# The first batch's attention with transposed scores, and its state read-out moved from slot 0 to slot 1

## The chip, the cores and the metric

One core of a Trainium2 chip runs the kernel. The metric is device time in microseconds (us). A profiled execution gives the span (first to last instruction), some 1.8 us under the device time. Engines: PE (matmul; PEld is its weight load), DVE (VectorE), ACT (ScalarE), POOL (GpSimd), SP (SyncE). A name with q, such as SPq, is that engine's instruction queue.

## The reference

Attention between 512 tokens and 32 state rows for each of 8 batches and 8 heads, in both directions, then a two-layer network with exact GELU over all 4,352 rows. It is cut to what matters:

```python
scores = scale * x @ state.T            # (B, H, 512, 32)
xread = softmax(scores, -1) @ state     # tokens read the state
sread = softmax(scores.T, -1) @ x       # the state reads the tokens: "read-out"
attn = concat([xread, sread], axis=2)   # (B, H, 544, 64); subtraction of maxima and 1e-9 left out
h = attn.transpose(0, 2, 1, 3).reshape(B * 544, 512) @ w_in      # 512 -> 2048
out = gelu_exact(h) @ w_out                                      # 2048 -> 512
```

## The kernel before

The kernel does not form `xread` by itself: it forms P = state · w_in for each batch, and the hidden layer is (normalised scores) · P. Both kinds of read share one set of exponentials `e`, laid out with tokens on the partitions: the normalised `a` is transposed to `AT` for the hidden products, and `e` itself is the left operand of the read-out `sr`. All 8 batches' read-outs go through the network together at the end. P is made piece by piece, as the pieces of w_in land; the products of its third piece are called the third P stretch. A row block is 128 rows of w_out.

Batch b's work on PE is called slot b. Weights come in pieces over GpSimd's one queue while slot 0 runs. What the change and the argument touch:

```python
    load_w_in(0, 512)            # two transfers (partition halves) of 256 KB
    load_w_out(0)                # first quarter of w_out, 512 KB
    load_w_in(512, 1024)
    load_st(1, 2)
    ...
    def load_rest():             # called later in the start
        load_x(1)
        load_w_out(1)            # second quarter
        for f in range(2, FC):
            load_w_in(512 * f, 512 * f + 512)
            load_w_out(f)
    ...
    def scores0(q):              # batch 0, two heads of each half at a time: tokens on partitions
        pc = ps_o.tile([128, SJ, 2 * NS], FP32, name="pc", tag="op")
        for j in range(SJ):
            nc.tensor.matmul(pc[:, j, :], lhsT=xT0[:, q, j, :], rhs=sb0[...], ...)
        nc.scalar.activation(out=part0(A.e, q), in_=pc, func=AF.Exp, scale=scale)
    # sums0: reduce_sum on DVE; norm0: reciprocal, then a = e * (1/sum) on GpSimd (t=0) or DVE (t=1);
    # atr(0): eight PE transposes of a, two copies to AT
    ...
    pmat00(0)                    # P, first piece: 4 products, ACT copies them
    nc.scalar.activation(out=gate, in_=gate, func=AF.Gelu)   # loads the GELU table early
    ...
    pmat00(1)
    ...                          # eight hidden products, four GELUs, then products with w_out
    # slot 0, later:
    M(6); begin(1); xtr(1, (0, 1)); xtr(1, (2, 3))
    sread(0)                     # read-out: 32 products of 32 columns
    sread_out(0)                 # reciprocal and multiplication on DVE
    M(7); scores(1, 0); scores(1, 1)
    srt(0)                       # transpose of the read-out
    U(4, 5)                      # first products that need w_out's second quarter
    ...
    # M(m): two hidden products and their GELU; U(u): four products with w_out.
    # Tile pools in PSUM: ps_f and ps_o, four buffers each; hidden products, score tiles and sr turn through ps_f.
    ...
        if q == 3:               # a finished tile of 128 rows: copied and stored
            rows = out_rows(b, j)
            h = d_model // 2 if j == SJ - 1 else d_model      # the last tile of a batch in two stores
            evac(ps, [(rows[:, n:n + h], slice(0, 128), n, n + h) for n in range(0, d_model, h)])
```

The softmax here doesn't subtract the row's maximum and nothing guards it: scores larger than these inputs give would overflow.

## Time and profile before

| | before |
|---|---|
| time, median of 3 runs | 215.44 us (215.35 to 215.75) |
| span of the profiled execution | 213.6 us |
| first GELU of batch 0 starts | 12.67 us |
| first product with w_out's second quarter | 21.18 us |
| slot 0 ends (score products of the batch after next start) | 44.16 us |
| slot 1 ends (the same of the batch after) | 57.58 us |
| last output tile's products start | 206.99 us |

How to read it. The last rows are times at which PE passes the same piece of work in every version. Differences between two kernels in the distance from one such milestone to the next tell in which stretch time was gained or lost. The line behind 21.18 stands in the prediction, those behind the other milestones in the result. The chains shown there date a group of products some 0.17 us later than the timeline, from which the milestones are taken, because a chain's piece starts where the one before it ends.

### The profile page before, as it was taken

What the parts mean: (1) busy time and instruction counts of PE and PEld (TensorE: products, weight loads), DVE (VectorE), ACT (ScalarE), POOL (GpSimd) and SP (SyncE); (2) the same over time, 40 slices, a digit from 0 to 9 for tenths busy, and PEclk for the clock granted to TensorE, in tenths of its full rate; (3) what the DMA queues carried; (4) which work ended last, traced back from release to release, by engine and by line L of the source; (5) the groups of instructions that cost most, each with busy time, mean ns of one, the idle gap of its engine ahead of it and who ended that gap; (6) DMA issues with size and microseconds to landing.
All of it is one profiled execution on the core that took longest, in us unless ns stands there. A gap on an engine that the chain in (4) does not pass through costs nothing.

```text
span 213.6 us, 4028 instructions
## 1 busy us (share of the span) xinstructions
PE 209.2 (98%) x1674; PEld 103.7 (49%) x1674; DVE 81.3 (38%) x169; ACT 122.5 (57%) x218; POOL 43.5 (20%) x57
## 2 busy tenths in 40 slices
PE   8999999999999999999999999999999999999994
PEld 7735444444444445444444444444444444765443
DVE  3835675723059102940177006900393026000151
ACT  3765855797777448844974467645864444864000
POOL 7573304901213013302321230300000000000000
PEclk9999999999999999999999999999999999999999
DMA  7999999983722691439350963170222014000034
GB/s 182 172 200 205 206 193 161 220 178 51 96 98 101 122 123 50 150 60 144 47 196 4 155 90 139 60 146 5 98 100 54 0 40 158 3 0 0 10 105 183
DMA packets 39731, 22.98 MB, mean 108 GB/s; under 512 B 22048, under 2 KB 36384, under 8 KB 39712
## 3 DMA queue, kind: packets, MB, share of 16 engines
q0 software_dynamic: 13664, 8.23, 27.8%
q1 hardware_dynamic: 25360, 14.09, 24.6%
q10 hardware_dynamic: 688, 0.39, 0.6%
q8 instruction: 13, 0.21, 0.4%
q14 instruction: 6, 0.05, 0.1%
HBM read 17.30 MB, written 8.91 MB: 123 GB/s over the span
## 4 chain that ended last, share of the span: by engine, by line
PE 97%; POOL 0%; ACT 0%; issue 0%; DVE 0%
PE op L519 47%; PE hp L470 25%; PE p_ps L408 4%; PE op L564 3%; PE hps L534 3%; PE ops L546 3%; PE warm_ps L133 2%; PE opl L497 2%; PE pt L316 2%; PE sr L371 1%; PE hp L624 1%; PE aT_ps L353 1%; PE xT_ps L239 1%; POOL a L303 0%; PE xT_ps L258 0%; PE pc L279 0%
## 5 line engine op out<-in xcount | busy, mean ns | idle before, releaser
L519 PE MATMUL op<-w_out_bf,g 128*128 128x512 bf16 x464 | 110.1, 379 | 0.0
L477 ACT ACTIVATE g<-hp 128x512 bf16<-128x512 f32 x124 | 66.5, 600 | 52.8 <-PE hp L470 52.7
L519 PEld LDWEIGHTS <-g 128*128 128x128 bf16 x464 | 44.9, 98 | 54.3 <-issue 1.5
L470 PE MATMUL hp<-AT,P 128*128 128x512 bf16 x248 | 63.4, 379 | 0.0
L483 DVE COPY osb<-op 128x512 f32<-128x512 f32 x31 | 21.4, 691 | 85.0 <-PE op L519 85.0
L470 PEld LDWEIGHTS <-P 128*128 128x128 bf16 x248 | 22.8, 98 | 25.2 <-ACT P L419 0.5
L419 ACT CAST P<-p_ps 128x512 bf16<-128x512 f32 x31 | 16.3, 595 | 12.5 <-PE p_ps L408 12.5
L420 DVE CAST P<-p_ps 128x512 bf16<-128x512 f32 x31 | 19.9, 682 | 6.0 <-PE p_ps L408 5.9
L202 POOL COPY x<-xb 128x1024 bf16<-128x1024 bf16 x12 | 12.2, 1043 | 31.9 <-DMA xb<-in_x_dram 26.5
L212 POOL COPY xo<-xb 128x1024 bf16<-128x1024 bf16 x12 | 12.2, 1049 | 21.7 <-PE sr L371 21.7
L336 DVE TENSOR_REDUCE cs<-e 128x16 f32<-128x512 bf16 x14 | 9.5, 678 | 4.0 <-ACT e L323 4.0
L323 ACT ACT_TABLE_LOAD x7 | 9.0, 1283 | 1.8 <-issue 1.3
L408 PE MATMUL p_ps<-w_in_bf,sbd 64*32 64x512 bf16 x248 | 9.9, 381 | 0.0
L483 DVE COPY osb<-ops 128x512 f32<-128x512 f32 x2 | 1.4, 692 | 22.5 <-PE ops L546 22.5
L339 DVE TENSOR_TENSOR a<-e,ics 128x512 bf16<-128x512 bf16 x14 | 9.7, 692 | 0.5
L477 ACT ACT_TABLE_LOAD x7 | 9.0, 1283 | 0.1
L508 ACT COPY osb<-opl 128x128 f32<-128x128 f32 x1 | 0.3, 266 | 15.2 <-PE opl L497 15.2
L133 PE MATMUL warm_ps<-warm 128*128 128x128 bf16 x66 | 7.0, 275 | 1.0 <-DVE warm L80 1.0
L564 PE MATMUL op<-w_out_bf,g 128*128 128x512 bf16 x32 | 7.8, 380 | 0.0
L323 ACT ACTIVATE e<-pt 128x512 bf16<-128x512 f32 x14 | 7.6, 594 | 0.1
L534 PE MATMUL hps<-XSR,w_in_bf 128*128 128x256 bf16 x64 | 7.6, 273 | 0.0
L546 PE MATMUL ops<-w_out_bf,g_sr 128*128 128x512 bf16 x32 | 7.1, 379 | 0.0
(80 smaller groups left out, 118.9 us busy)
## 6 DMA issues: line engine op xcount, KB each, us to landing
out_dram<-osb SPq DMA_DIRECT2D x24, 256.0 KB, 2.3
xb<-in_x_dram POOLq DMA_DIRECT2D x7, 512.0 KB, 6.2
w_in_bf<-in_moe_w_in_dram POOLq DMA_DIRECT2D x8, 256.0 KB, 10.1
w_out_bf<-in_moe_w_out_dram POOLq DMA_DIRECT2D x4, 512.0 KB, 11.6
out_dram<-osb SPq DMA_DIRECT2D x14, 128.0 KB, 2.0
x0f<-in_x_dram SPq DMA_DIRECT2D x2, 256.0 KB, 3.5
out_dram<-osb SPq DMA_DIRECT2D x8, 64.0 KB, 1.7
x0f<-in_x_dram ACTq DMA_DIRECT2D x1, 256.0 KB, 4.2
```

The source lines that it names most:

```text
L202: nc.gpsimd.tensor_copy(out=A.x4[:, :, :, 64 * t:64 * t + 64].rearrange("p j c d -> p c j d"), in_=src[:, t],)
L323: nc.scalar.activation(out=A.e[:, :, 64 * half:64 * half + 64], in_=pt.rearrange("p j t c n -> p (j t) (c n)"), func=AF.Exp, scale=scale,)
L408: nc.tensor.matmul(ps[t][32 * c:32 * c + 32, :], lhsT=sbd[64 * t:64 * t + 64, b, c, 32 * t:32 * t + 32], rhs=w_in_bf[64 * t:64 * t + 64, c ...
L419: nc.scalar.copy(out=dst[:, 0, :], in_=ps[0])
L420: nc.vector.tensor_copy(out=dst[:, 1, :], in_=ps[1])
L470: nc.tensor.matmul(hp, lhsT=Ps[b][:, t, m * 128:(m + 1) * 128], rhs=atts[b].AT[:, :, t, :], start=(t == 0), stop=(t == 1),)
L477: nc.scalar.activation(out=gs[b][:, m, :], in_=hp, func=AF.Gelu)
L483: nc.vector.tensor_copy(out=osb, in_=ps)
L519: nc.tensor.matmul(ps, lhsT=gs[b][:, m, j * 128:(j + 1) * 128], rhs=w_out_bf[:, m, :], start=(m == 0), stop=(m == MC - 1),)
L534: nc.tensor.matmul(hp, lhsT=w_in_bf[:, c, m * 128:(m + 1) * 128], rhs=XSR[:, c, :], start=(c == 0), stop=(c == HC - 1),)
L546: nc.tensor.matmul(ps, lhsT=g_sr[:, m, s * 128:(s + 1) * 128], rhs=w_out_bf[:, m, :], start=(m == 0), stop=(m == MC - 1),)
L564: nc.tensor.matmul(ops[b, j], lhsT=gs[b][:, m, j * 128:(j + 1) * 128], rhs=w_out_bf[:, m, :], start=(m == 0), stop=(m == MC - 1),)
```

## The change

Its intent: shorten the way to the first hidden product. Batch 0's scores are computed with state rows on the partitions, which is the layout the hidden products want, so that the GpSimd normalisation, the eight transposes and two copies go. Sums come from products with a 0/1 matrix and are spread again by 32 broadcast products for each half of the heads. The read-out still wants tokens on partitions: its operand now comes from a DMA transpose of the exponentials, and the read-out moves to slot 1. The first piece of w_in comes in four transfers instead of two, and the casts and copies of x go to DVE.

```diff
-    load_w_in(0, 512)
+    load_w_in(0, 256, (0,))
+    load_w_in(256, 512, (0,))
+    load_w_in(0, 256, (1,))
+    load_w_in(256, 512, (1,))
     load_w_out(0)
@@ scores0: one product of 512 columns for each q, one exp for each pair
-        for j in range(SJ):
-            nc.tensor.matmul(pc[:, j, :], lhsT=xT0[:, q, j, :], rhs=sb0[...], ...)
-        nc.scalar.activation(out=part0(A.e, q), in_=pc, func=AF.Exp, scale=scale)
+        nc.tensor.matmul(pcs[t][h, :], lhsT=sb0[...], rhs=xT0[:, q, :, :]..., ...)
+        if q % 2 == 1:
+            nc.scalar.activation(out=eT0[:, t, :], in_=pcs[t], func=AF.Exp, scale=scale)
@@ sums0: four products with the 0/1 matrix, reciprocal, its low part
+            nc.tensor.matmul(ps[:, j, :], lhsT=eT0[:, t, 128 * j:128 * j + 128], rhs=bones, ...)
+        nc.vector.reciprocal(out=r0[:, t, :, :], in_=ps)
+        nc.vector.tensor_tensor(out=r0lo[...], in0=r0[...], in1=r0_hi(t), op=ALU.subtract)
@@ norm0: for each half 32 broadcast products, one multiplication from PSUM
+                    nc.tensor.matmul(ps[...], lhsT=r[:, j, c:c + 1].to_broadcast((128, NS)), rhs=ident, ...)
+        nc.vector.tensor_tensor(out=A.AT[:, :, t, :], in0=eT0[...], in1=ps..., op=ALU.mult)
+    def e0_dma():
+        nc.sync.dma_start_transpose(out=e0, in_=eT0.rearrange("p t s -> p (t s)"))
@@ start
+    load_rest()                  # now behind the scores, some 2 us sooner
     sums0(0)
+    pmat00(0)
+    nc.scalar.activation(out=gate, in_=gate, func=AF.Gelu)
     sums0(1)
     norm0(0)
     norm0(1)
     pmat00(1)
@@ slot 0
-    sread(0)
-    sread_out(0)
     M(7)
     scores(1, 0)
     scores(1, 1)
-    srt(0)
@@ behind batch 2's transpose, before slot 1
     xtr_dma(2)
+    e0_dma()
@@ slot 1, p == 4, behind the next batch's scores
+                    sread(0)
+                    sread_out(0)
@@ slot 1, p == 5
+                srt(0)
```

Left out: the removed lines of sums0, norm0, atr(0) and of the old start, the order of warm-up products, copies moved between ACT and DVE, new buffers, and the index of `e` in `sread`.

More of the change, by code (lines that the diff above doesn't have):

```diff
@@ L64 @@
     sb0 = persist.tile([128, 2, 2, 2, NS], BF16, name="sb0")
+    e0 = persist.tile([128, 2 * SJ, 128], BF16, name="e0")
+    eT0 = persist.tile([128, 2, S], BF16, name="eT0")
+    xo0 = persist.tile([128, SJ, HC, 132], BF16, name="xo0")
+    bones = persist.tile([128, HC], BF16, name="bones")
+    r0 = persist.tile([128, 2, SJ, HC], FP32, name="r0")
+    r0lo = persist.tile([128, 2, SJ, HC], BF16, name="r0lo")
     gate = persist.tile([128, HC], FP32, name="gate")
@@ L85, with load_w_in @@
     nc.vector.memset(sb0, 0.0)
-    for i in range(2):
-        nc.vector.memset(xos[i][:, :, :, 1:2], 1.0)
-        nc.vector.memset(xos[i][:, :, :, 130:131], 1.0)
-    def load_w_in(f0, f1):
-        for t in range(2):
+    nc.vector.memset(bones, 0.0)
+    for c in range(HC):
+        nc.vector.memset(bones[32 * c:32 * c + 32, c:c + 1], 1.0)
+    for xo in xos + [xo0]:
+        nc.vector.memset(xo[:, :, :, 1:2], 1.0)
+        nc.vector.memset(xo[:, :, :, 130:131], 1.0)
+    def load_w_in(f0, f1, ts=(0, 1)):
+        for t in ts:
             nc.gpsimd.dma_start(
@@ L127, in load_rest, with keep_warm @@
         load_x(3)
-    def keep_warm(n):
-        ps = ps_o.tile([128, 512], FP32, name="warm_ps", tag="op")
+    warm_ps = ps_o.tile([128, 512], FP32, name="warm_ps", tag="op")
+    def keep_warm(n, m=128):
         for _ in range(n):
-            nc.tensor.matmul(ps[:, 0:128], lhsT=warm, rhs=warm, start=True, stop=True)
+            nc.tensor.matmul(
+                warm_ps[0:m, 0:128], lhsT=warm[:, 0:m], rhs=warm, start=True, stop=True
+            )
     def state_prep(b0, b1):
@@ L171, in state0 @@
             h = slice(64 * u, 64 * u + 64)
-            nc.vector.tensor_copy(out=sb0[h, :, :, u, :], in_=ps[h, 0:2, u:HC:2, :])
+            nc.scalar.copy(out=sb0[h, :, :, u, :], in_=ps[h, 0:2, u:HC:2, :])
         return ps
@@ L189, in begin @@
         A.x4 = x4s[b % 2]
-        A.xo = xos[b % 2]
-        if b > 0:
-            A.xT = att.tile([128, SJ, HC, 128], BF16, name="xT", tag="xT")
+        A.xo = xos[b % 2] if b else xo0
+        if b == 0:
+            A.e = e0
+            A.AT = att.tile([128, SJ, 2, 128], BF16, name="AT", tag="AT")
+            return
+        A.xT = att.tile([128, SJ, HC, 128], BF16, name="xT", tag="xT")
         A.e = att.tile([128, SJ * 2, HC * NS], BF16, name="e", tag="e")
@@ L218, in cast0 @@
     def cast0(q):
-        copy = nc.scalar.copy if q == 1 else nc.vector.tensor_copy
-        copy(
+        nc.vector.tensor_copy(
             out=x0b[:, q, :, :, :].rearrange("p j u d -> p u j d"),
@@ L246, in xtr0 @@
                 )
-        copy = nc.scalar.copy if q == 2 else nc.vector.tensor_copy
-        copy(out=xT0[:, q, :, :], in_=ps)
+        nc.vector.tensor_copy(out=xT0[:, q, :, :], in_=ps)
     def xtr(b, cs):
@@ L268, in xtr_dma, with sums0 @@
         )
-    def part0(x, q):
-        v = x.rearrange("p (j t) f -> p j t f", t=2)[:, :, q // 2, :]
-        return v[:, :, 64 * (q % 2):64 * (q % 2) + 64]
+    pcs = {}
     def scores0(q):
-        A = atts[0]
-        pc = ps_o.tile([128, SJ, 2 * NS], FP32, name="pc", tag="op")
+        t = q // 2
+        if q % 2 == 0:
+            pcs[t] = ps_o.tile([128, S], FP32, name="pc", tag="op")
+        h = slice(64 * (q % 2), 64 * (q % 2) + 64)
+        nc.tensor.matmul(
+            pcs[t][h, :],
+            lhsT=sb0[:, t, q % 2, :, :].rearrange("p u n -> p (u n)"),
+            rhs=xT0[:, q, :, :].rearrange("p j n -> p (j n)"),
+            start=True,
+            stop=True,
+        )
+        if q % 2 == 1:
+            nc.scalar.activation(out=eT0[:, t, :], in_=pcs[t], func=AF.Exp, scale=scale)
+    def sums0(t):
+        ps = ps_f.tile([128, SJ, HC], FP32, name="cs0", tag="f")
         for j in range(SJ):
             nc.tensor.matmul(
-                pc[:, j, :],
-                lhsT=xT0[:, q, j, :],
-                rhs=sb0[:, q // 2, q % 2, :, :].rearrange("p u n -> p (u n)"),
+                ps[:, j, :],
+                lhsT=eT0[:, t, 128 * j:128 * j + 128],
+                rhs=bones,
                 start=True,
@@ L285, in scores0, with r0_hi @@
             )
-        nc.scalar.activation(out=part0(A.e, q), in_=pc, func=AF.Exp, scale=scale)
-    def sums0(q):
-        A = atts[0]
-        if q % 2 == 0:
-            A.sums = att.tile([128, SJ, HC], FP32, name="cs", tag="cs")
-        nc.vector.reduce_sum(
-            out=A.sums[:, :, q % 2 * 2:q % 2 * 2 + 2],
-            in_=part0(A.e, q).rearrange("p j (c n) -> p j c n", n=NS),
-            axis=AX.X,
-        )
+        nc.vector.reciprocal(out=r0[:, t, :, :], in_=ps)
+        nc.vector.tensor_tensor(
+            out=r0lo[:, t, :, :], in0=r0[:, t, :, :], in1=r0_hi(t), op=ALU.subtract
+        )
+    def r0_hi(t):
+        v = r0.rearrange("p t j c -> p (t j c)").bitcast(BF16)
+        return v.rearrange("p (t j c w) -> p t j c w", t=2, j=SJ, w=2)[:, t, :, :, 1]
     def norm0(t):
         A = atts[0]
-        ics = att.tile([128, SJ, HC], FP32, name="ics", tag="ics")
-        nc.vector.reciprocal(out=ics, in_=A.sums)
-        eng = nc.gpsimd if t == 0 else nc.vector
-        eng.tensor_tensor(
-            out=A.a.rearrange("p (j t) (c n) -> p j t c n", t=2, n=NS)[:, :, t, :, :],
-            in0=A.e.rearrange("p (j t) (c n) -> p j t c n", t=2, n=NS)[:, :, t, :, :],
-            in1=ics[:, :, :].to_broadcast((128, SJ, HC, NS)),
+        ps = ps_o.tile([128, S], FP32, name="rb", tag="op")
+        for j in range(SJ):
+            for i, r in enumerate((r0_hi(t), r0lo[:, t, :, :])):
+                for c in range(HC):
+                    nc.tensor.matmul(
+                        ps[32 * c:32 * c + 32, 128 * j:128 * j + 128],
+                        lhsT=r[:, j, c:c + 1].to_broadcast((128, NS)),
+                        rhs=ident,
+                        start=(i == 0),
+                        stop=(i == 1),
+                    )
+        nc.vector.tensor_tensor(
+            out=A.AT[:, :, t, :],
+            in0=eT0[:, t, :].rearrange("p (j n) -> p j n", j=SJ),
+            in1=ps.rearrange("p (j n) -> p j n", j=SJ),
             op=ALU.mult,
         )
+    def e0_dma():
+        nc.sync.dma_start_transpose(out=e0, in_=eT0.rearrange("p t s -> p (t s)"))
     def scores(b, half):
@@ L372, in sread @@
                         A.sr[32 * c:32 * c + 32, t, :],
-                        lhsT=A.e[:, 2 * j + t, 32 * c:32 * c + 32],
+                        lhsT=A.e[:, 2 * j + t if b else SJ * t + j, 32 * c:32 * c + 32],
                         rhs=A.xo[:, j, c, 1 + 65 * t:66 + 65 * t],
@@ L583 @@
     cast0(0)
+    xtr0(0)
     st0 = state0()
-    xtr0(0)
     cast0(1)
     state0_p(st0)
-    keep_warm(7)
+    keep_warm(9)
     cast0(2)
     xtr0(1)
+    keep_warm(2)
+    xtr0(2)
+    xtr0(3)
     scores0(0)
-    xtr0(2)
-    keep_warm(4)
     scores0(1)
+    keep_warm(1, 64)
+    scores0(2)
+    keep_warm(2, 64)
+    scores0(3)
+    load_rest()
     sums0(0)
-    xtr0(3)
-    keep_warm(2)
-    scores0(2)
-    keep_warm(4)
+    pmat00(0)
+    nc.scalar.activation(out=gate, in_=gate, func=AF.Gelu)
     sums0(1)
     norm0(0)
-    scores0(3)
-    sums0(2)
-    sums0(3)
     norm0(1)
-    load_rest()
-    keep_warm(8)
-    pmat00(0)
-    nc.scalar.activation(out=gate, in_=gate, func=AF.Gelu)
-    keep_warm(5)
-    atr(0, (0,))
-    keep_warm(4)
     pmat00(1)
-    atr(0, (1,))
     for q in range(4):
@@ L723 @@
                 srt(b)
+            if p == 5 and b == 1:
+                srt(0)
     while u < 16 * B - 4:
```

## The prediction

> **What bounds the kernel now.** I read the busy shares first, then the chain that ended last, then the order of time of the first 25 us, then the DMA issues in short windows. From the page:
>
> ```profile
> PE 209.2 (98%) x1674; PEld 103.7 (49%) x1674; DVE 81.3 (38%) x169; ACT 122.5 (57%) x218; POOL 43.5 (20%) x57
> ...
> PE 97%; POOL 0%; ACT 0%; issue 0%; DVE 0%
> ```
>
> PE is the bound from beginning to end: after the start every microsecond that PE neither loses nor gains elsewhere arrives at the end. So the change is worth (a) how much earlier the first batch's hidden products begin, (b) waits that it adds or removes on PE later. The chain of waits, from 8 us on:
>
> ```profile
> 8.77 0.39 ACT e L286
> 9.16 1.05 POOL a L303
> 10.21 0.05 issue
> 10.25 0.40 PE aT_ps L353 x4
> ...
> 11.53 1.75 PE hp L624 x8
> ...
> 18.75 1.01 PE xT_ps L258 x32
> 19.77 0.36 PE sr L371 x31
> 20.12 0.54 PE hp L470 x2
> 20.66 0.47 PE pt L316 x16
> 21.13 0.21 PE srT L395
> ```
>
> The only stretch not carried by PE is 8.77 to 10.25: the last exp, then GpSimd's normalisation (1.05). That is what the change attacks. But a second path runs beside it, on ACT, in the order of time:
>
> ```profile
> 9.55 0.59 ACT L460 CAST P<-p_ps 128x512 bf16<-128x512 f32 x1 [0.40 <-PE p_ps L453]
> ...
> 10.16 1.28 ACT L609 ACT_TABLE_LOAD   x1
> ...
> 11.45 0.20 ACT L609 ACTIVATE gate<-gate 128x4 f32<-128x4 f32 x1
> 11.56 0.57 ACT L460 CAST P<-p_ps 128x512 bf16<-128x512 f32 x1
> ```
>
> The second P copy ends at 12.13; the second half of the eight hidden products loads its weights at 12.18, released by that copy. So ACT (P copy, GELU table, P copy) is already as late as the attention path, and stays after it.
>
> The third thing to see is the load stream. Every weight comes over GpSimd's one queue, busy without a break to 37 us. The output projection's second quarter is issued at 11.10 and takes 10.0 us:
>
> ```profile
> w_out_bf<-in_moe_w_out_dram POOLq DMA_DIRECT2D x1, 512.0 KB, 10.0
> ...
> 21.18 1.02 PE L519 MATMUL op<-w_out_bf,g 128*128 128x512 bf16 x4
> 21.42 0.99 POOL L104 DMA_DIRECT2D xb<-in_x_dram  x1 [1.92 <-DMA w_out_bf<-in_moe_w_out_dram]
> ```
>
> It lands at 21.14; its first product starts at 21.18. PE was ready just then by itself, so it costs nothing today, but there is no slack: whatever PE gains before 21 us it will spend waiting here. By the same arithmetic other slacks are: first quarter of w_out 12.2 against 13.3, second piece of w_in 15.3 against 16.0, batch 1's x 18.2 against 18.7, third piece 23.3 against 23.9.
>
> **What the Trainium skill says.** "ScalarE: Activation LUTs", section "What ACT_TABLE_LOAD costs", gives about 1283 ns for a load, whatever the set, and 186 ns + 0.833 ns a column for an ACTIVATE. The trace agrees: 1283 ns a load, 597 ns for 512 columns (613 by that formula), 388 for 256. Two exps of 512 columns thus cost 1.2 us where four of 256 cost 1.6. "TensorE: Matmul & The Clock Gate", "Part 3: Packing small matmuls — row/col tiling", says that products of 32 columns in different column groups overlap; here 32 read-out products start within 0.24 us (19.70 to 19.93), so it agrees. The same page's "Part 1: The HAM clock gate" puts the warm clock after some 4 us of activity and its loss after an idle window of about 3.4 us; here products of 128 columns go from 107 to 56 ns apart near 6.6 us, and the new gaps are all well under a microsecond, so I expect no cold stretch. "DMA: Bandwidth & Descriptors", "Specifications", has 512 B as the least size for line rate. The trace shows a small loss even there, by stretch:
>
> ```profile
> 19.00:23.00 4.00, 4.00 (x88) 2.57 (x83) 2.92 (x7) 2.72 (x4) 2.08 (x3) 1.00 1.24 205
> 32.40:34.60 2.20, 2.20 (x11) 0.84 (x9) 0.00 (x0) 1.30 (x3) 0.00 (x0) 1.00 1.46 200
> 5.50:8.20 2.70, 2.70 (x45) 2.48 (x44) 2.00 (x6) 1.92 (x6) 1.10 (x2) 1.00 1.10 146
> ```
>
> The last number is GB/s. The first stretch moves 1024-byte packets at 205; the second 512-byte packets, at 191 when the 0.02 MB of instruction fetch is left out.
>
> **The change, part by part.** Times are the span's.
>
> *Scores transposed.* Sixteen products of 64 columns become four of 512 (216 ns each warm, from the hidden products' spacing). x's transposes come first on PE (4.38 instead of 4.9), all casts and transposed copies go to DVE at 0.42 each. DVE in order: cast 0 to 4.27, copy 0 5.05 to 5.48, cast 1 to 5.91, cast 2 to 6.35, copy 1 6.89 to 7.31 (after nine warm-up products at 107 ns), copy 2 to 7.75, copy 3 to 8.19. First exp from 7.87 to 8.45; the fourth score product needs copy 3, starts at 8.26 and ends at 8.64; second exp 8.67 to 9.25. Before, the last exp ended at 9.15: nothing gained yet.
>
> *Sums and normalisation.* Four products for the sums (0.3), reciprocal 0.25, subtraction about 0.1, 32 broadcast products (eight steps of 56 ns, 0.45, plus 0.17 until they have landed), one multiplication from PSUM 0.7. First half: sums done 8.95, reciprocal and low part 9.35, broadcast 9.6 to 10.25, multiplied 10.97. Second half: sums 9.3 to 9.6, low part 10.0, broadcast 10.1 to 10.7, multiplied 11.7. The GpSimd pass (1.05), eight transposes (0.8) and two copies (0.84) go.
>
> *ACT.* The first P copy can start at 9.28, when the second exp ends, instead of 9.55. Then 0.59, table 1.28, gate 0.11 before the copy may follow, copy 0.57: end at 11.86 instead of 12.13. The first four hidden products run 11.0 to 11.9, the second four from 11.95. **The start gains 0.27 us**, set by ACT; attention at 11.7 lies just under it.
>
> *Read-out moved.* Leaves slot 0 with 0.36 + 0.21 of the chain. There, though, the second score tile then waits for the second transposed copy of x (0.68 on DVE), so about 0.3 is freed.
>
> *The w_in split.* Four loads of 512-byte rows for two of 1024: 524 kB at 191 instead of 205 GB/s is 2.75 for 2.56 us, +0.2 on every later landing. GpSimd's issues rise by 2 x 0.63 us, and the rest is issued about 2 us sooner; both are hidden, as the queue is never empty.
>
> *Put together at w_out's second quarter.* PE would be ready 0.3 + 0.27 earlier, at about 20.6; the data lands at 21.14 + 0.2 = 21.34, products at 21.38. So slot 0 ends **+0.2 us**, its 0.57 gained turned into a wait.
>
> *Read-out in slot 1.* After 44 us PE is full, so it is paid: 0.36 for the 32 products and 0.06 for the transpose (0.06 is what that costs in later slots, where it waits for nothing). It also takes a PSUM buffer of the four that the hidden products turn through. Score tiles hold two until exp, which sits behind a table load:
>
> ```profile
> 44.64 1.28 ACT L323 ACT_TABLE_LOAD   x1 [0.37 <-PE pt L316]
> ...
> 45.93 1.08 ACT L323 ACTIVATE e<-pt 128x512 bf16<-128x512 f32 x2
> ```
>
> The second hidden product of that step therefore needs the read-out's own buffer or a score tile's. If it is the read-out's: products land about 45.13, reciprocal 0.16 and multiplication 0.29 with gaps to 45.66, PE ready at 45.4 and starting at 45.7: a wait of about 0.25. **Sum for slot 1: 0.36 + 0.06 + 0.25 = +0.65.** The DMA transpose of e is issued near 39 us and should take the 3.2 us of its like of the same eight blocks, so it lands near 42.5, before 44.7; stores behind it have time.
>
> *Total.* +0.2 + 0.65 = +0.85; on 215.44 that is 216.3. I take 216.2, as the kernel's author kept such a step presumably for a reason.
>
> **Rivals.**
> 1. *The gain stands.* If the first loads come faster split than whole, w_out lands sooner. For it: the stretch 5.5 to 8.2 moves only 146 GB/s, 0.16 MB or 0.8 us behind the later rate, and it is exactly the piece that is split. Against: nothing in the profile says that packet size is the reason. Then slot 0 ends up to 0.5 earlier, total about 215.5 to 215.7.
> 2. *The score tile's buffer is taken.* Then the hidden product waits for the first exp, 46.53 + 0.05, against 45.41: 1.15 instead of 0.25, total about 217.2. For it: the tiles turn over in order. Against: in the compiled kernel before, slot 0's transposed read-out gives its bank on before the older score tiles do, so banks follow the expected release.
> 3. *A slower load stream.* If small rows also lengthen that slow stretch, landings slip by 0.5 or more, and each of the near deadlines becomes a wait: about 216.7 to 217.
> 4. *Attention sets the start instead of ACT*, if the broadcast products or the multiplications from PSUM run longer: hidden up to 0.5 us by the same w_out wait.
>
> **Range and chances.** Rival 1 with a smaller slot 1 gives the low side, 215.2; rival 2 or 3 the high side, 217.2. Two per cent is 4.3 us, beyond any sum of these: faster 0.01, within 0.975, slower 0.015.
>
> **What would show it.** Second P copy ending near 11.9, first GELU near 12.4 instead of 12.67; the first L519-like products with g of batch 0 and the second quarter of w_out starting within 0.1 us of its landing, with PE idle before; read-out products near 45 followed by a wait of a quarter microsecond before the second hidden product; PE busy about 0.5 us lower in slot 0. It is wrong if w_out's landing moves by more than 0.4 us either way, if PE's wait in slot 1 ends with an exp, or if the clock falls in the start.

## More of the kernel before

Differences of a few tenths of a microsecond are near the spread of single runs (the kernel before, on one chip, lay between 214.95 and 216.69 in eleven runs), so the argument rests on intervals of repeated rounds for the times and on profiles for the places.

## The result

| | before | changed |
|---|---|---|
| time, median | 215.59 us (215.35 to 215.99, 4 runs) | 216.58 us (216.40 to 216.82, 4 runs) |
| span of the profiled execution | 213.6 us | 215.0 us |

The ratio is 1.0045, 95% interval 1.0025 to 1.0064. Ratios in this document are the mean time of one kernel's fast runs over that of the kernel before in the same rounds, so they are not quite the ratios of the medians. The changed kernel's profiled run was the slowest of its four; its milestones run some 0.4 us late against the repeat below, the first product with w_out's second quarter 0.85.

First the page of the changed kernel, the chain that ended last, by engine:

```profile
PE 88%; DMA 6%; POOL 3%; issue 1%; DVE 0%; ACT 0%; POOLq 0%
```

Before, this line began with 97% for PE. Now 6% of the span, some 12.5 us, is a DMA: the chain goes back from the first product with w_out's second quarter to that transfer, and from there to GpSimd's issues of the loads in front of it. By this chain no work of PE, ACT or DVE before 21 us is on the path any more. The timeline of the changed kernel shows both ends of that statement, first on ACT (start, length, line, operation; in brackets the idle time before it and what ended it), then on PE, with the issue-to-landing time of the transfer from the list of DMA issues in the third fence. The fourth is the kernel before's first GELU:

```profile
9.74 1.28 ACT L643 ACT_TABLE_LOAD   x1
...
11.14 0.57 ACT L500 CAST P<-p_ps 128x512 bf16<-128x512 f32 x1
...
12.19 2.06 ACT L665 ACTIVATE g<-hp 128x512 bf16<-128x512 f32 x4 [0.48 <-PE hp L657]
```

```profile
21.33 2.75 PE L559 MATMUL op<-w_out_bf,g 128*128 128x512 bf16 x11 [0.48 <-DMA w_out_bf<-in_moe_w_out_dram]
```

```profile
w_out_bf<-in_moe_w_out_dram POOLq DMA_DIRECT2D x1, 512.0 KB, 12.5
```

```profile
12.67 2.06 ACT L632 ACTIVATE g<-hp 128x512 bf16<-128x512 f32 x4 [0.54 <-PE hp L624]
```

The table load starts 0.42 earlier (9.74 for 10.16), the second P copy ends at 11.71 for 12.13, and the first GELU starts 0.48 earlier. Then PE waits 0.48 for w_out's second quarter. It was issued 2.35 us earlier than before (8.75 for 11.10), took 2.5 us longer and landed 0.14 later, at 21.28.

The second place is slot 1. The chain of waits of the changed kernel there, then that of the kernel before (start, length, what):

```profile
44.52 0.47 PE pt L356 x16
44.98 0.41 PE sr L411 x32
...
45.41 0.18 DVE inv L424
...
45.62 0.30 DVE srm L425
...
45.97 0.60 PE hp L510 x2
...
58.72 0.47 PE pt L356 x16
```

```profile
44.32 0.47 PE pt L316 x16
44.79 0.86 PE hp L470 x4
...
57.74 0.47 PE pt L316 x16
```

From one score tile to the next it is now 14.20 us, and was 13.42. The chain leaves PE for 0.53 us: the read-out's products, the reciprocal and the multiplication on DVE, and only then the second hidden product. The timeline of the changed kernel names what that product waits for:

```profile
45.96 0.11 PEld L510 LDWEIGHTS <-P 128*128 128x128 bf16 x2 [0.58 <-DVE srm L425]
```

After the last output tile's products have begun, the kernel before ends within 6.57 us and the changed one within 7.05, though the same instructions lie between. The lines show where these products begin; the spans are 213.56 and 215.02:

```profile
206.99 3.66 PE L497 MATMUL opl<-w_out_bf,g 128*128 128x384 bf16 x32
```

```profile
207.97 3.66 PE L537 MATMUL opl<-w_out_bf,g 128*128 128x384 bf16 x32
```

The SyncE queue's waits tell where (total, times, longest), before and then changed:

```profile
SPq L756 <- DMA out_dram<-osb: 1.4, 2, 1.1
```

```profile
SPq L791 <- DMA out_dram<-osb: 1.9, 1, 1.9
```

These are the waits at the end of the program, for the stores. They last 0.5 us longer.

Milestones of the two profiles, and the same of the changed kernel profiled again:

| us | before | changed | changed again | length before | length changed |
|---|---|---|---|---|---|
| first GELU | 12.67 | 12.19 | 11.83 | | |
| product with w_out's 2nd quarter | 21.18 | 21.33 | 20.48 | 8.51 | 9.14 |
| slot 0 ends | 44.16 | 44.35 | 43.93 | 22.98 | 23.02 |
| slot 1 ends | 57.58 | 58.55 | 58.13 | 13.42 | 14.20 |
| last tile's products | 206.99 | 207.97 | 207.55 | 149.41 | 149.42 |
| end | 213.56 | 215.02 | 214.61 | 6.57 | 7.05 |

Slots 2 to 7 are equal to 0.01 us. So the loss is 0.78 in slot 1 and 0.48 at the end; slot 0 lies between -0.2 and +0.2 of before, depending on when the weights landed. The sum, with slot 0 at its two values, is 1.05 and 1.45; the times say 0.99. From slot 0's end to the end of the span it takes 169.4 us in all four profiles with the old start, and 170.66 to 170.70 in the five with the new start and the read-out where the change put it (changed, e0, e2, e3, e6). So these executions differ, but for 0.04 us, only in what happened before slot 0's end.

### The profile page after: what moved, and what is told of

Read it like the earlier page. It is cut to its first block, busy times and chain, and to the rows that moved or that the text cites. A ratio compares the mean times of both kernels' runs of the same rounds, so it can differ in the third digit from the quotient of the medians.

```text
span 215.0 us, 4068 instructions
## 1 busy us (share of the span) xinstructions
PE 208.4 (97%) x1681; PEld 103.2 (48%) x1706; DVE 80.1 (37%) x173; ACT 121.7 (57%) x216; POOL 43.6 (20%) x58
## 4 chain that ended last, share of the span: by engine, by line
PE 88%; DMA 6%; POOL 3%; issue 1%; DVE 0%; ACT 0%; POOLq 0%
PE op L559 46%; PE hp L510 24%; DMA w_out_bf<-in_moe_w_out_dram 6%; PE p_ps L448 4%; PE hps L574 3%; PE ops L586 3%; POOL w_in_bf L101 2%; PE opl L537 2%; PE op L604 2%; PE sr L411 1%; PE pt L356 1%; POOL xb L113 0%; POOL x0c L85 0%; POOL w_out_bf L109 0%; POOL st_bf L117 0%
## 5 line engine op out<-in xcount | busy, mean ns | idle before, releaser
L559 PE MATMUL op<-w_out_bf,g 128*128 128x512 bf16 x441 | 107.8, 379 | 1.7 <-DMA w_out_bf<-in_moe_w_out_dram 0.5
L604 PE MATMUL op<-w_out_bf,g 128*128 128x512 bf16 x30 | 7.6, 380 | 0.1
L574 PEld LDWEIGHTS <-w_in_bf 128*128 128x128 bf16 x64 | 6.3, 98 | 1.6
```

The source lines that it names most:

```text
L559: nc.tensor.matmul(ps, lhsT=gs[b][:, m, j * 128:(j + 1) * 128], rhs=w_out_bf[:, m, :], start=(m == 0), stop=(m == MC - 1),)
L574: nc.tensor.matmul(hp, lhsT=w_in_bf[:, c, m * 128:(m + 1) * 128], rhs=XSR[:, c, :], start=(c == 0), stop=(c == HC - 1),)
```

## The experiments

Theories after the result. **A (the loads):** the start gains, but slot 0 cannot end sooner than the weights land. **B (slot 1):** the read-out costs its own products plus a wait for its own buffer. **C (the end):** the added DMA transpose costs 0.48 at the very end. Rivals: a gain of the start that is lost to the split of w_in (so that whole transfers would do better); a transpose that would be hidden anyway, so that the read-out should stay in slot 0; and for the end, chance. All kernels ran, five rounds each, against the kernel before in the same rounds. C was found by laying the milestones of all profiles side by side; its test is the last run.

| run | ratio, 95% interval | median, us | slot 1, us | last tile to end, us |
|---|---|---|---|---|
| e0 changed again | 1.0052, 1.0028 to 1.0076 | 216.59 | 14.20 | 7.06 |
| e1 read-out later | 1.0035, 1.0010 to 1.0060 | 216.12 | 13.94 | 7.03 |
| e2 w_out in halves | 1.0049, 1.0028 to 1.0070 | 216.59 | 14.20 | 7.04 |
| e3 changed, no wait for w_out's 2nd quarter (wrong result) | 1.0041, 1.0019 to 1.0063 | 216.28 | 14.24 | 7.03 |
| e4 before, no wait for it (wrong result) | 1.0008, 0.9975 to 1.0042 | 215.85 | 13.41 | 6.55 |
| e5 read-out in slot 0 | 1.0093, 1.0064 to 1.0123 | 217.70 | 13.42 | 7.04 |
| e6 w_in whole | 1.0045, 1.0016 to 1.0074 | 216.69 | 14.19 | 7.05 |
| e7 whole, later, halves, new order | 1.0085, 1.0048 to 1.0122 | 217.35 | 13.93 | 7.05 |
| f1 changed: later, halves, order kept | 1.0028, 1.0013 to 1.0043 | 216.06 | 13.94 | 7.02 |
| f2 before, w_in split | 0.9989, 0.9973 to 1.0004 | 215.14 | 13.42 | 6.55 |
| f3 before: split, halves, order of f1 | 0.9984, 0.9966 to 1.0002 | 215.25 | 13.42 | 6.57 |
| g1 f1 with one store less | 1.0004, 0.9980 to 1.0029 | 215.74 | 13.94 | 6.62 |

The kernel before had medians of 215.41, 215.49, 215.31 and 215.57 (e0 to e3, e4 to e7, f1 to f3, g1).

**e0. The changed kernel again**, unaltered.

> The changed kernel once more, as the yardstick for the other runs of this chip. My theory and every rival: about 1.0 us above the kernel before (216.6 against 215.5), ratio 1.004 to 1.006; w_out's second quarter lands near 21.3 and its first product waits about 0.5 us for it; in slot 1 the second hidden product of the step with the read-out waits 0.25 to 0.3 us for the vector engine.

It confirms the ratio and shows the spread of slot 0: here w_out's second quarter lands sooner, its first product starts at 20.48, and PE stands next at the third piece of w_in (23.65). Slot 1 and the end are as in the first profile. The first GELU starts 0.36 sooner than in the first profile. One reason lies in PE: its nine warm-up products of 128 columns still ran some 107 ns apart in the first profile and 56 ns apart here, as these lines of the two timelines show:

```profile
5.38 1.17 PE L146 MATMUL warm_ps<-warm 128*128 128x128 bf16 x9
```

```profile
5.24 0.67 PE L146 MATMUL warm_ps<-warm 128*128 128x128 bf16 x9
```

The slow pace lasted beyond 6 us in three profiles (before, changed, e7) and ended between 4.0 and 5.5 us in the other eleven. Starts are compared at like pace below.

**e1. The read-out later**, where eight hidden products and sixteen products with w_out stand between score tiles and read-out.

```diff
                 if b == 1:
-                    sread(0)
-                    sread_out(0)
                     norm(nb, 0)
...
             if p == 5 and b == 1:
+                sread(0)
+                sread_out(0)
+            if p == 7 and b == 1:
                 srt(0)
```

> The changed kernel with batch 0's read-out moved behind the second projections of the next step of slot 1, where no score tile waits in PSUM, and its transpose one step pair later. My theory: the 32 products still cost 0.36 us, but the wait for the read-out's buffer goes, so 0.25 to 0.35 us less than the changed kernel: ratio to before about 1.003. Rival A (the buffer is not the cause, the place of 0.3 us is the switch between tile shapes, which stays): within 0.1 us of the changed kernel. Rival B (the added DMA transpose and the stores behind it cost the time): no change either.

Slot 1 falls from 14.20 to 13.94. The chain of e1 shows hidden products right behind the score tile, with no DVE between:

```profile
44.01 0.47 PE pt L356 x16
44.47 0.86 PE hp L510 x4
```

So 0.26 of slot 1's 0.78 is the wait for the buffer and 0.52 the read-out's own work on PE: in e1's chain 0.36 for its products, 0.06 for its transpose, and some 0.1 because the four hidden products right behind it took 0.97 and not 0.86 (why was not looked into). Part B stands. The times agree (1.0035 for 1.0052), though the intervals overlap.

**e2. w_out's second quarter in two transfers**, its products in the order of landing.

```diff
-        load_w_out(1)
+        load_w_out(1, 0, 2)
+        load_w_out(1, 2, 4)
...
-    U(4, 5)
+    mm2_m(0, 4)
+    mm2_m(0, 5)
     rearr_ones(1)
-    U(6)
+    mm2_m(0, 6)
...
-    U(7)
+    mm2_m(0, 7)
```

> The changed kernel with w_out's second quarter loaded as two halves of two row blocks, and the four products of each output tile of that quarter taken row block by row block over all four tiles, so that the first eight need the first half alone. The count of products is the same. My theory (the 0.48 us that the start gained went into the wait for this load): the first half lands near 19.9, the first product starts near 20.7 instead of 21.33, and up to 0.4 us is kept, unless the third piece of w_in (landing 23.3 to 24.0) takes it again at 23.3; total 0.1 to 0.45 us under the changed kernel. Rival (PE was not really waiting for this load, the profile's releaser is a coincidence): no change, 21.3 again.

The first of these products starts at 20.45, without a wait. Then the next weights are missing. The timeline of e2:

```profile
20.45 2.75 PE L606 MATMUL op<-w_out_bf,g 128*128 128x512 bf16 x12
...
24.14 0.41 PE L450 MATMUL p_ps<-w_in_bf,sbd 64*32 64x512 bf16 x7 [0.62 <-DMA w_in_bf<-in_moe_w_in_dram]
```

The wait moved from w_out to the third piece of w_in, and the ratio did not move. That fits theory A: the stream, not one transfer, is what slot 0 runs against.

**e3 and e4. Without the wait for w_out's second quarter**, in the changed kernel and in the one before. Half of its first products read the first quarter instead, which gives a wrong result (relative error 0.203).

```diff
-                rhs=w_out_bf[:, m, :],
+                rhs=w_out_bf[:, m - 4 if b == 0 and q == 1 and j < 2 else m, :],
```

> Wrong results on purpose: the changed kernel, whose first eight products of w_out's second quarter read the first quarter instead, which landed long before. Loads, their order and all else are as in the changed kernel. My theory: these products start near 20.7 instead of 21.33, PE reaches the third P stretch near 23.4, and there waits until the third piece of w_in has landed (22.2 and 23.3 to 24.0), so the gain at the end is between 0 and 0.5 us; the trace must show the wait gone at one place and, if the total stays, come back at the other. Rival (the wait for w_out is no real limit): same start, same total.

> Wrong results on purpose: the kernel before with the same edit (the first eight products of w_out's second quarter read the first quarter). My theory: there PE came to this point just when the load landed, so nothing changes: within 0.15 us of the kernel before, first product at 21.18 again, as the transposed read-out ahead of it is what it waits for. Rival (the load held the kernel before as well): 0.2 us or more faster.

Both are inside the spread of their originals: 1.0041 against 1.0052, and 1.0008 against 1. In e4's profile slot 0 ended 0.7 later than before, because the loads were late in that execution: PE waited 1.06 at 14.03 for w_out's first quarter, which landed at 13.99 and not at 12.24. So e4 decides little by itself. In e3's profile these products start at 20.61 without a wait, and PE stands at the third piece of w_in instead (reached at 23.29, landed at 23.41). e3's median is 0.3 under e0's, so removing this one wait is worth at most a few tenths.

**e5. The read-out back in slot 0**, with the DMA transpose issued right behind the scores.

```diff
     scores0(3)
+    e0_dma()
     load_rest()
...
     xtr(1, (2, 3))
+    sread(0)
+    sread_out(0)
     M(7)
     scores(1, 0)
     scores(1, 1)
+    srt(0)
```

and the three calls in and before slot 1 taken out.

> The changed kernel with the read-out back in slot 0 and the DMA transpose of batch 0's exponentials issued right behind the second exp, near 9.2 us, in the middle of the weight loads. The results stay right. My theory: slot 1 loses its 0.7 to 0.8 us; in slot 0 the products (0.36) fall into PE's wait for w_out; but the transpose moves a quarter of a megabyte through the engines that the loads keep full, so every landing behind it moves by 0.3 to 1.3 us and PE waits that much longer: total between 0.5 us under and 0.6 us over the changed kernel, with w_out's second quarter landing at 21.3 or later, about 21.9. Rival (a transpose between on-chip buffers does not slow the loads): landings as before, total 0.75 us under the changed kernel, about 215.8.

Slot 1 is as before the change (13.42), and the kernel is still the slowest of all, 0.93% over the kernel before. That is 1.1 us over e0, in another call; the theory had at most 0.6. In the list of DMA issues the transpose took 3.5 us in the changed kernel and 9.6 in e5:

```profile
e<-eT SPq DMA_TRANSPOSE x1, 3.5
```

```profile
e<-eT SPq DMA_TRANSPOSE x1, 9.6
```

It runs amid the weights and slows them. The stretch from 14 to 16 us, before and then e5 (the last number is GB/s):

```profile
14.00:16.00 2.00, 2.00 (x10) 0.77 (x8) 0.00 (x0) 0.74 (x2) 1.02 (x2) 1.00 1.50 193
```

```profile
14.00:16.00 2.00, 1.88 (x14) 0.59 (x12) 0.00 (x0) 0.00 (x0) 0.30 (x2) 1.00 1.45 158
```

Of e5's 0.32 MB in these 2 us, only 0.18 MB (some 90 GB/s) are on the weights' queue; before, all 0.39 MB were. Batch 1's x lands at 19.65 (17.9 to 18.9 in the other profiles), w_out's second quarter lets its first product start at 22.22, and slot 0 ends at 45.81. So with the transpose issued here, amid the loads, the read-out is better off in slot 1. No other place for the transpose was tried.

**e6. w_in's first piece whole again**, the rest of the change kept.

```diff
-    load_w_in(0, 256, (0,))
-    load_w_in(256, 512, (0,))
-    load_w_in(0, 256, (1,))
-    load_w_in(256, 512, (1,))
+    load_w_in(0, 512)
```

> The changed kernel with the first piece of w_in loaded by two transfers again and not by four. My theory (rows of 512 bytes move 7% slower): later landings 0.1 to 0.2 us earlier, the total 0 to 0.2 us under the changed kernel. Rival 1 of the prediction (the split relieves the slow stretch between 5.5 and 8.2 us): landings later and total 0.2 to 0.6 us over the changed kernel.

The time doesn't tell between the theory and its rival (1.0045 with an interval of 0.6%). The profile does: the first P product waits 0.93 us for w_in and starts at 9.13 (8.69 and 8.33 in the two profiles of the changed kernel), and the first GELU starts at 12.63, where it was before the change:

```profile
9.13 0.40 PE L490 MATMUL p_ps<-w_in_bf,sbd 64*32 64x512 bf16 x4 [0.93 <-DMA w_in_bf<-in_moe_w_in_dram]
```

So in this execution the start's gain was lost without the split: attention was ready and w_in wasn't. That it always is lost isn't shown: the first P product needs the first half of the piece, which landed between 8.26 and 9.09 in the four profiles with w_in whole and between 7.47 and 8.00 in nine of the ten with it split (8.76 in g1), and in e7, whole too, it was there at 8.26, before attention asked for it. The stretch from 6 to 7 us in three kernels: before, changed, and f2, which is the kernel before with nothing but the split:

```profile
DMA packets 111, 0.11 MB, mean 113 GB/s; under 512 B 1, under 2 KB 111, under 8 KB 111
```

```profile
DMA packets 317, 0.15 MB, mean 154 GB/s; under 512 B 16, under 2 KB 317, under 8 KB 317
```

```profile
DMA packets 284, 0.14 MB, mean 137 GB/s; under 512 B 17, under 2 KB 284, under 8 KB 284
```

Smaller packets, and more bytes; over all profiles it is 137 to 177 GB/s in the ten with the split and 100 to 113 in the four without. Across the profiles the last part of the first piece landed between 8.87 and 9.41 when split (10.13 in g1, where a load in front of it was late) and between 9.54 and 10.37 when whole. Whether the shorter rows do it or the smaller transfers was not separated.

**e7. Everything together**: w_in whole, the read-out later, w_out in halves, and the products around it in a new order. The diff shows the order, on top of e1, e2 and e6.

```diff
     mm2_m(0, 6)
-    pmat(0, 2)
+    mm2_m(0, 7)
     norm(1, 0)
+    pmat(0, 2)
+    sread(1)
     norm(1, 1)
-    mm2_m(0, 7)
     M(8, 9)
-    sread(1)
     sread_out(1)
```

> The changed start with what the experiments point to: first piece of w_in whole, w_out's second quarter in halves and taken row block by row block, the third P stretch behind the last products of that quarter with batch 1's read-out as filler while its copies run, and batch 0's read-out later in slot 1. My theory: of the 0.5 us that the start gained and the 0.15 us that the kernel before lost behind its transposed read-out, 0.3 us is left over by a wait for the P copies; the total is 0.1 to 0.4 us under the kernel before, 215.0 to 215.3, ratio 0.998 to 0.9995. Rival (the load stream sets this stretch whatever the order on PE): no better than the kernel before, 215.4 to 215.9.

It failed: 1.0085. In the profile PE waits 0.68 at 27.54 for batch 1's read-out on DVE, which my new order had put behind a normalisation, and 0.35 at 25.39 for a P copy. I had made new waits while filling old ones. f1 is the mended form.

**f1, f2, f3. The repairs in both kernels.** f1 is the changed kernel with e1 and e2, and with batch 1's read-out two steps sooner so that PE has work until w_in's third piece lands. f3 makes the same repairs in the kernel before (with the split, and without moving batch 0's read-out, which is in slot 0 there). f2 is the kernel before with the split alone. The diff shows what f1 adds to e1 and e2.

```diff
     mm2_m(0, 6)
+    sread(1)
+    sread_out(1)
     pmat(0, 2)
     norm(1, 0)
     norm(1, 1)
     mm2_m(0, 7)
     M(8, 9)
-    sread(1)
-    sread_out(1)
     M(10, 11)
```

> The last try mended: changed start, first piece of w_in in four transfers, w_out's second quarter in halves and taken row block by row block, batch 1's read-out and its division ahead of the third P stretch, batch 0's read-out later in slot 1. In the last try the score of batch 1's division stood behind a normalisation and held a PSUM buffer for 0.7 us; here it is ahead of it. My theory (load stream and PSUM buffers are all that the start's gain is lost to): the third P stretch starts between 23.5 and 24.1, no wait over 0.2 us on a buffer, slot 1 0.5 us longer than in the kernel before, total 215.2 to 215.7, so equal to the kernel before within 0.15%. Rival (the load stream leaves nothing): 216.0 to 216.3, as with the later read-out alone.

> The kernel before with the first piece of w_in loaded by four transfers, nothing else. The traces so far show the second half of this piece landing at 8.9 to 9.4 where it is in four transfers and at 9.5 to 10.4 where in two. New theory (against the prediction's step that the split costs 0.2 us): the landing moves 0.5 us or more ahead here too, with 5 to 15 packets of over 200 ns before 9 us instead of 40 to 50; the total is within 0.3 us of the kernel before, as its start is bound by the attention path. The step as predicted: landings 0.2 us later.

> The kernel before with the split, the halves of w_out's second quarter and batch 1's read-out ahead of the third P stretch, its own start and its read-out in slot 0 kept. It differs from f1 by the start and the place of batch 0's read-out alone. My theory: its PE has nothing to win at w_out, the read-out moved ahead fills no wait; within 0.3 us of the kernel before, and 0 to 0.4 us under f1, as f1 pays 0.5 us in slot 1 for a start of which the loads leave it 0.1 to 0.5 us. Rival (the new start is worth its 0.5 us once the order is mended): f1 is 0.2 us or more ahead of this one.

The start first, by all profiles: the first GELU begins on the mean at 12.52 in the kernel before (two profiles), at 12.50 with the new attention and w_in whole (two), at 12.25 with the old attention and w_in split (two), and at 12.02 with both (eight, g1 included, from 11.83 to 12.59). These means mix causes: PE's pace (above), a late w_in (e6, and 0.19 in e4) and a late x (e2, g1). At like pace and with nothing late, the new attention's first GELU starts 0.48 sooner (12.19 for 12.67) where the pace rose late, and 0.3 to 0.5 sooner where it rose early (11.83 to 11.87 in e0, e1, e3, e5 and f1, against 12.15 in f3 and 12.35 in f2). In e7, with w_in whole and the pace rising late, it starts at 12.37, 0.30 before the kernel before. So the attention does gain at the start by itself, by these single profiles, and a late w_in can take that gain away, as in e6.

f1's profile, of its fastest run, ends slot 0 at 43.56, 0.6 before the original (at f1's median, 0.34 slower, it would be some 0.3), with no wait at w_in's third piece (its P products start at 23.61, behind the moved read-out). The theory's total for f1 (215.2 to 215.7) failed: 216.06 is where its rival put it. f1 is still 0.44% above f3, 0.95 us, where 0 to 0.4 was expected. Slot 1 (0.52) and the end (0.45, 7.02 against 6.57) make 0.97. So no gain of the new attention in slot 0 shows against the old one with the same loads, which fits theory A; but the two intervals leave this open by some 0.5 us either way (an estimate from their widths). f3's profile can't settle it, as it is of its slowest run. f2 and f3 lie 0.1 to 0.2% under the kernel before, with intervals that include 1; they are not shown to be faster. In f2 the first piece landed at 9.39, 0.24 before the kernel before's and not 0.5 or more as expected (0.7 before e4's). Packets of over 200 ns between 2.5 and 9 us were 15, against 49 in the kernel before, near what was expected.

**g1. One store less.** In the compiled kernels the DMAs that SyncE and ScalarE issue take one of eight semaphores in turn, and the program ends with SyncE waiting for these eight in a fixed order. Counted from the lists of DMA issues there are 64 such DMAs before (48 stores, 4 loads, 12 transposes) and 65 in the changed kernel. With 64 the last store has the eighth semaphore, and the seven waits in front of it are done while the store is under way. With 65 it has the first, and seven waits come after it. The trace's records of these waits, which come when a wait is over, counted from the end of ACT's last copy: in the changed kernel the store's own at 1.75 us, the others at 1.81, 1.88, 1.94, 2.00, 2.06, 2.12 and 2.18, some 0.06 apart; before, the store's was the last, at 1.70. g1 is f1 with the two stores of one tile in batch 3 made one, which gives 64 again:

```diff
-            h = d_model // 2 if j == SJ - 1 else d_model
+            h = d_model // 2 if j == SJ - 1 and b != 3 else d_model
```

> f1 with one pair of half stores in the middle of the kernel (batch 3) made one store, so that the DMAs issued by the sync engine and ACT are 64 again as in the kernel before, and not 65 as in every kernel with the added DMA transpose. New theory: these DMAs take turns on eight semaphores, and the sync engine waits for the eight in a fixed order at the end; with 65 the last store's is the first in that order, and seven further waits of about 0.06 us come after it, with 64 it is the last. So from the start of the last output tile's products to the end of the span it takes 6.55 to 6.6 us, as in the four profiles with 64, and not 7.0 to 7.06 as in the eight with 65; the total is 0.4 to 0.5 us under f1, 215.55 to 215.7, ratio about 1.001. Rival (the longer end has another cause, such as more stores late in the kernel): 7.0 us again, total as f1, ratio 1.003.

From the last tile to the end it takes 6.62 instead of 7.02, and SyncE's wait has its old form:

```profile
SPq L795 <- DMA out_dram<-osb: 1.5, 2, 1.1
```

The ratio went from 1.0028 (f1) to 1.0004; the two ran on different chips, each against the kernel before. Theory C stands by the profile: a store taken out at some 110 us, 100 us before the end, changes the end by 0.4 us. No count but 64 and 65 was run.

No version was shown to beat the kernel before. The best form of the change (g1) can't be told from it.

## Why the prediction was right or wrong

The total was right (216.2, measured 216.58, in its range), with a sum of +0.85 against +0.99 by the first medians and 0.52%, 1.1 us, in the repeat. PE's granted clock stayed at 1.0, as expected; but the change of pace from 107 to 56 ns, which the prediction dates near 6.6 us, came between 4.0 and 7.0 us in the 14 profiles. By its steps:

- **"The start gains 0.27 us", set by ACT: right in the mechanism, too small.** ACT's order is as said: exp, P copy, table, gate, P copy without a gap. The copy ended at 11.71, not 11.86, as the second exp ended at 9.10 and not 9.25; the first GELU started 0.48 earlier in this profile (0.84 in e0's, but there the pace rose sooner than in the kernel before's). Attention's second multiplication ended at 11.38 (11.7 was predicted), so rival 4 did not come true. It made little difference to the end, because of the next step.
- **"Data lands at 21.34, products at 21.38": right in this profile** (21.28 and 21.33; PE waited 0.48), and with it "its gain turned into a wait", which e2, e3 and f1 against f3 bear out. The closeness is luck: in the repeat the load landed at 20.43 and the product started at 20.48. By the prediction's own sign (a landing that moves by more than 0.4) this step fails there; the landings of one program spread more than the step allowed.
- **"+0.2 on every later landing" by the split: wrong.** The first piece landed sooner when split, and in e6, without it, the start's gain was lost. Later landings were no later either: w_out's second quarter landed at 20.4 to 22.0 in nine profiles with the split (e5 aside), 21.0 on the mean, and at 21.0 to 21.6 in four without, 21.2 on the mean (the last half, where it came in two). The step took the later stretches' rate for each packet size and put it on a stretch with a different limit; the 146 GB/s in 5.5 to 8.2, which rival 1 named, was the better witness (167 in the same stretch after the change). Rival 1 was right about this first piece, but its conclusion, that slot 0 would end up to 0.5 earlier and the total be 215.5 to 215.7, did not follow: further gates (w_out, then w_in's third piece) took most of it.
- **Slot 1, "0.36 + 0.06 + 0.25 = +0.65": right in the mechanism, too small.** Its own terms make 0.67; 0.78 was measured. The buffer awaited is the read-out's own, not a score tile's, so rival 2 fell. e1 separates the terms: 0.26 for the wait, as predicted, and 0.52 for the work where 0.42 was put. The missing 0.1 is the slower hidden products behind the read-out.
- **Missing: the end, +0.48.** The prediction counted the added transpose's own time and the stores behind it, but not that one DMA more shifts the turns of the semaphores on which the program's end waits. g1 showed it.
- **"I take 216.2, as the kernel's author kept such a step presumably for a reason": had no evidence** and went the wrong way. The sum itself, 216.3, was closer.

So the total came out near by luck, because two errors of about equal size, the missing end (+0.48) and slot 0's +0.2, which by the times was a gain of 0.1 to 0.3, pulled against each other. What stays open: slot 0's exact share, since a weight's landing differs by up to 0.9 us between runs of the same program (21.33 and 20.48 for the first product with w_out's second quarter), and why the split loads the first piece faster.

## What to carry to other kernels

When the weights land just in time, a faster start buys only a longer wait; read the landing of every later transfer before valuing it. Place added work where no tile that turns over in PSUM waits behind it: some 5 us further on, the same read-out cost 0.26 less. Before comparing the starts of two profiles, check that PE ran at the same pace in both and that the same loads were there. And compare the stretch after the last product too: here one DMA more or less, 100 us before the end, moved it by 0.4 us.

## What the Trainium skill lacked or had wrong

- No page that I read gives the end of a program as a cost that depends on the number of DMAs: with 64 DMAs on SyncE and ScalarE the last tile took 6.55 to 6.62 us to the end in five profiles of different kernels, with 65 it took 7.02 to 7.06 in nine, by seven more waits of about 0.06 us each.
- "DMA: Bandwidth & Descriptors", section "Why small descriptors are slow (HBM only)", counts a fixed overhead for each packet. The later stretches agree in direction (205 GB/s with 1024-byte packets, 191 with 512), but the start does not follow from it: from 6 to 7 us, packets of about 512 B moved 137 to 177 GB/s in ten profiles and packets of about 1 KB 100 to 113 in four. The page has nothing on what limits such a stretch. (The number of transfers changed too, so row length alone is not shown to be the cause.)
- "Advanced Engine Details and Errata", section "X-Bar Transpose (TRN2)", has transposes as fast as ordinary DMAs. Here 256 KB took 3.5 us from issue to landing late in slot 0 (3.5 to 4.2 in nine profiles), against the 2.3 us median of a 256 KB store, and 9.6 us amid the weight loads, whose rate fell from 193 to some 90 GB/s in 14 to 16 us. The page does not say what a transpose costs the loads beside it.
